# A state-space convolution gated by a GLU, forward and gradients: 8 KB pieces of SBUF for all phases, the down product over all channels in one pass, its gradient transposed at once, part of the weight transposes moved forward

## The chip, the cores and the metric

The kernel runs on one core of one Trainium2 chip. The time is the device time of one execution in microseconds (us), given as the median of three runs. A profile, with a trace of every instruction, comes from one further execution. The engines are named as the profile does: PE (matrix products), DVE (elementwise), ACT (activations, copies, casts), POOL (elementwise work and issuing stores and the convolution's loads) and SP (issuing the other loads).

## The reference

Everything is for one sequence of S = 2048 positions, D = 1024 channels, F = 3584 hidden features, in bf16. The output is computed, and the gradients of nine inputs for a given grad_out.

```
xn = layernorm(x)                                  # x is A_q
kv = shift_conv(k, shift_k) * v                    # four taps per channel
y  = irfft(rfft(kv, 2S) * rfft(ssm_k, 2S))[:S]     # long convolution per channel
s  = xn * (y + kv * ssm_D)
bm = ((xn @ w_gate) * (xn @ w_up)) @ w_down
out = x + s * silu(bm)
out, vjp = jax.vjp(f, x, k, v, shift_k, ssm_k, ssm_D, w_gate, w_up, w_down)
grads = vjp(grad_out)
```

## The kernel before

The sequence is cut into 16 blocks of 128 rows, the channels into 8 pieces of 128, the features into 28 pieces (fc), two of which make a slab of 256. The long convolution is a Fourier transform written out as matrix products with cosine tables (TF, TFO, TI, from `build_tables`) and elementwise combinations on DVE. It is written as a generator that hands out small units of work, each with an estimated cost; `make_pump` gives a `pump` that takes units until their sum has reached a given fraction of the total, and the product loops call it at every tick. So the convolution runs inside the dense products, at a pace set by counts. Loads go out on SP's queue in the order of the program (`ld`), stores and the convolution's loads on POOL's (`st`, `cld`). Tiles come from pools; a tile whose place is still in use makes its first writer wait.

The stages, with the times that they take in the profiled execution:

- 0 to 187 us: layer norm of the blocks in pieces of 1, 1, 2, 4, 4 and 4 (`layer_norm`, L396; its transposes L438 go through one PSUM buffer, copied by ACT or DVE as the scheduler picks, L439, to XNT). After each group of four blocks (q) follow the gate and up products of fc 0 to 3 (`gu_unit`, L442; product psg L452, casts to gut L454). Then `build_tables` (L140): integer angles, two Sin activations L159 for each of eight pieces, and 64 transposes L166 with copies L167.
- 187 to 706: `gu_unit` for fc 4 to 27, in two halves each. Each unit stores gut to GUTd, multiplies its halves to hT on DVE, stores hT to HTd, and at once transposes hT (L465), copies it (L467) and stores it to Hd. `conv_forward` is pumped inside, and leaves y in YFd.
- 706 to 728: the last unit's hT, w_down's loads, the first ht from HTd.
- 728 to 958: the down product (psbm, L781) in two passes over halves of the channels, so that HTd is read twice; the gating behind it computes the output, dbm (gradient of bm, stored to DBMd), dy and dxa. In the second pass `dy_forward` (transform of dy) is pumped to 7% of the backward convolution. The gradient dD is a product beside it (psd, L826).
- 958 to 1048: w_down is loaded as wrow and transposed (L864); DBMd is loaded again, block by block, and transposed to DBMT (`load_dbmt`, L868 to L874).
- 1048 to 1783: for each slab four `dh_half` (product psdh L886, dht L888, dgt = gul times dht on DVE, stored to DGUTd; its transposes L897 at once, copies L898 to dgu), and `dw_slab` (psdw L904, wb L908, out). `conv_backward` is pumped by `btick`.
- 1783 to 2022: gradient of w_down from Hd and DBMd (psdw L947), the rest of the backward convolution pumped inside.
- 2022 to 2143: w_gate and w_up are loaded as wn and transposed (`build_wgu`, L979 to L989), seven pairs of pieces, each followed by its part of the first two blocks of dx (psx L1000).
- 2143 to 2486: the other 14 blocks of dx (psx) and layer norm's gradient.

## Time and profile before

| what | us |
|---|---|
| median of three runs | 2481.09 (2480.47 to 2485.43) |
| profiled execution | 2487.35 |
| its span, from first to last instruction | 2485.6 |
| PE busy | 2242.7 |
| DVE busy | 1445.3 |
| ACT busy | 859.8 |
| POOL busy | 626.6 |

The mean granted clock of PE is 0.967 of full speed. The profiled execution is 0.25% longer than the median, so that a duration of the trace may be read beside the runs' times as it stands. In a row of waits, the engine and the instruction that waited stand left of the arrow, what released it right of it, and then the sum, the number and the longest of these waits. In a row of groups the columns are line, engine, operation, tiles and count, then busy time and the mean of one in ns, then the idle time before them and its releaser.

### The profile page before, as it was taken

What the parts mean: (1) busy time and instruction counts of PE and PEld (TensorE: products, weight loads), DVE (VectorE), ACT (ScalarE), POOL (GpSimd) and SP (SyncE); (2) the same over time, 40 slices, a digit from 0 to 9 for tenths busy, and PEclk for the clock granted to TensorE, in tenths of its full rate; (3) what the DMA queues carried; (4) which work ended last, traced back from release to release, by engine and by line L of the source; (5) the groups of instructions that cost most, each with busy time, mean ns of one, the idle gap of its engine ahead of it and who ended that gap; (6) DMA issues with size and microseconds to landing.
All of it is one profiled execution on the core that took longest, in us unless ns stands there. A gap on an engine that the chain in (4) does not pass through costs nothing.

```text
span 2485.6 us, 35847 instructions
## 1 busy us (share of the span) xinstructions
PE 2242.7 (90%) x14634; PEld 1190.7 (48%) x14634; DVE 1445.3 (58%) x1935; ACT 859.8 (35%) x1204; POOL 626.6 (25%) x963
## 2 busy tenths in 40 slices
PE   3778999999979894799999999999999978999997
PEld 1335566666634442545454555444554434444443
DVE  6348979796855585526966775676674531322212
ACT  4573444444422221533343443345432112311111
POOL 2352223222213332022344344422213310000000
PEclk9889999999989997899999999999999989999999
DMA  8335656645569998534566665644747556433221
GB/s 244 130 117 207 223 189 208 200 164 177 195 229 331 325 324 223 182 130 164 181 211 217 205 213 184 199 155 158 278 150 233 181 163 204 161 122 140 103 101 34
DMA packets 217541, 469.55 MB, mean 189 GB/s; under 512 B 37488, under 2 KB 126616, under 8 KB 205344
## 3 DMA queue, kind: packets, MB, share of 16 engines
q0 software_dynamic: 71392, 265.92, 31.0%
q1 hardware_dynamic: 141824, 199.25, 25.2%
q8 instruction: 114, 1.87, 0.3%
q10 hardware_dynamic: 4160, 2.10, 0.3%
q14 instruction: 51, 0.42, 0.0%
HBM read 277.36 MB, written 194.02 MB: 190 GB/s over the span
## 4 chain that ended last, share of the span: by engine, by line
issue 37%; PE 30%; DVE 14%; DMA 9%; POOL 7%; ACT 3%; POOLq 0%; SPq 0%; DVEq 0%; ACTq 0%
PE psdw L904 12%; PE psbm L781 4%; PE psdw L947 4%; DVE W L179 4%; PE psdh L886 2%; POOL out_dram L60 2%; DMA wrow<-DBMd 2%; PE tr L897 1%; DVE m L179 1%; DVE dgt L179 1%; POOL HTd L60 1%; DMA DGUTd<-dgt 1%; DMA B<-HFd 1%; DVE HX L179 1%; PE psg L452 1%
## 5 line engine op out<-in xcount | busy, mean ns | idle before, releaser
L452 PE MATMUL psg<-XNT,wslab 128*128 128x512 bf16 x1792 | 417.8, 387 | 4.4 <-ACT XNT L439 4.4
L904 PE MATMUL psdw<-dgu,XN 128*128 128x512 bf16 x1792 | 402.6, 379 | 0.0
L1000 PEld LDWEIGHTS <-dgut 128*128 128x128 bf16 x1792 | 174.9, 98 | 222.2 <-DMA dgut<-DGUTd 15.2
L452 PEld LDWEIGHTS <-wslab 128*128 128x128 bf16 x1792 | 174.0, 100 | 198.6 <-issue 20.8
L904 PEld LDWEIGHTS <-XN 128*128 128x128 bf16 x1792 | 172.2, 98 | 192.1 <-issue 0.3
L60 POOL DMA_DIRECT2D out_dram<-wb x280 | 152.4, 551 | 274.0 <-ACT wb L908 198.8
L886 PE MATMUL psdh<-DBMT,wdt 128*128 128x512 bf16 x896 | 217.0, 386 | 2.6 <-ACT dht L888 1.5
L179 DVE TENSOR_TENSOR W<-W 128x512 f32<-128x512 f32 (+1 forms) x272 | 213.2, 784 | 7.1
L781 PE MATMUL psbm<-wd,ht 128*128 128x512 bf16 x896 | 203.2, 384 | 8.9 <-DMA ht<-HTd 6.6
L454 ACT CAST gut<-psg 128x512 bf16<-128x512 f32 x224 | 131.3, 587 | 214.8 <-PE psg L452 210.9
L947 PE MATMUL psdw<-DBMT,dgu 128*128 128x512 bf16 x896 | 198.4, 379 | 6.3 <-ACT wb L950 6.2
L179 DVE TENSOR_TENSOR W<-W,psP 128x512 f32<-128x512 f32 x192 | 122.5, 682 | 123.3 <-PE psP L228 76.2
L1000 PE MATMUL psx<-WGU,dgut 128*128 128x512 bf16 x768 | 169.5, 379 | 0.0
L908 ACT CAST wb<-psdw 128x512 bf16<-128x512 f32 x112 | 65.7, 587 | 247.0 <-PE psdw L904 210.8
L898 ACT COPY dgu<-tr 128x1024 bf16<-128x1024 bf16 x112 | 113.4, 1012 | 100.0 <-PE tr L897 99.4
L179 DVE TENSOR_TENSOR dxn<-psx,dxna_t 128x1024 f32<-128x1024 f32 x16 | 19.6, 1224 | 217.9 <-PE psx L1000 217.8
L947 PEld LDWEIGHTS <-dgu 128*128 128x128 bf16 x896 | 87.5, 98 | 110.4 <-issue 9.2
L781 PEld LDWEIGHTS <-ht 128*128 128x128 bf16 x896 | 87.3, 99 | 110.2 <-issue 7.4
L1000 PE MATMUL psx<-XN,dgut 128*128 128x512 bf16 x512 | 117.9, 387 | 14.4 <-DMA dgut<-DGUTd 14.4
L886 PEld LDWEIGHTS <-wdt 128*128 128x128 bf16 x896 | 85.2, 99 | 88.4 <-issue 7.6
L179 DVE TENSOR_TENSOR dgt<-gul,dht 128x2048 bf16<-128x2048 bf16 x56 | 68.3, 1220 | 98.9 <-ACT dht L888 93.4
L179 DVE TENSOR_TENSOR m<-A,B 128x2048 bf16<-128x2048 bf16 x64 | 75.8, 1221 | 85.4 <-DMA B<-KFd 40.8
(216 smaller groups left out, 3128.8 us busy)
## 6 DMA issues: line engine op xcount, KB each, us to landing
ht<-HTd SPq DMA_DIRECT2D x16, 1792.0 KB, 7.8
gul<-GUTd SPq DMA_DIRECT2D x56, 512.0 KB, 4.8
DGUTd<-dgt POOLq DMA_DIRECT2D x56, 512.0 KB, 5.9
dgut<-DGUTd SPq DMA_DIRECT2D x8, 3584.0 KB, 11.9
GUTd<-gut POOLq DMA_DIRECT2D x48, 512.0 KB, 3.7
A<-DYFd POOLq DMA_DIRECT2D x16, 1024.0 KB, 5.6
out_dram<-wb POOLq DMA_DIRECT2D x224, 64.0 KB, 2.1
dgu<-Hd SPq DMA_DIRECT2D x28, 512.0 KB, 4.7
```

What stands on the lines that cost most here:

```text
L60: return nc.gpsimd.dma_start(out=out, in_=in_)
L179: V.tensor_tensor(o, a, b, op)
L452: nc.tensor.matmul(ps[:], w[:, dc, a, fi * P:(fi + 1) * P], XNT[q][:, dc, :], start=(dc == 0), stop=(dc == DC - 1))
L454: nc.scalar.copy(out=gut[:, a, k * 512:(k + 1) * 512], in_=ps[:])
L781: nc.tensor.matmul(ps[:], ht[:, fc, i * P:(i + 1) * P], wds[fc // 4][:, fc % 4, :], start=(fc == 0), stop=(fc == NF - 1))
L886: nc.tensor.matmul(ps[:], wdt[:, dc, fi * P:(fi + 1) * P], DBMT[:, dc, s0:s0 + 512], start=(dc == 0), stop=(dc == DC - 1))
L897: nc.tensor.transpose(ps[:, i, :], dgt[:, a, i * P:(i + 1) * P], ident[:])
L898: nc.scalar.copy(out=dgu[:, :, a, fi * P:(fi + 1) * P], in_=ps[:])
L904: nc.tensor.matmul(ps[:].rearrange("p a f -> p (a f)"), XN[:, b, dc * P:(dc + 1) * P], dgus[b // 8][:, b % 8].rearrange("p a f -> p (a f)" ...
L908: nc.scalar.copy(out=wb[:], in_=ps[:])
L947: nc.tensor.matmul(ps[:], h[:, fi, b, :], DBM[:, b, dh * 512:(dh + 1) * 512], start=(b == 0), stop=(b == NB - 1))
L1000: nc.tensor.matmul(ps[:, dh * 512:(dh + 1) * 512], t[:, a, 4 * j + f, i * P:(i + 1) * P], WGU[j][:, a, f, dh * 512:(dh + 1) * 512], start= ...
```

## The change

Memory: four pieces of 8 KB a partition (U0 to U3) stand through the kernel, seven more (U4 to U10) from the end of the gate and up products on. XNT, the seven pieces of w_down, DBMT, XN, dgu, DBM and the transposed weights are all views of them, where each phase had its own pool.

Start: the loads of x all go out ahead of the copies KSLd<-k; layer norm's transposes have four PSUM buffers and their copies are DVE's; the tables are built beside the units of q = 1, from one Sin, one Abs and one Sin for each piece instead of two Sins and an integer mask; the second half of the products of fc 24 to 27 is done as a group.

Transposes of hT (and, later, of dgt) are put off: they are kept in a list and written out by `flush` behind the next product.

Down product: both halves of the channels in one pass, two matmuls for each weight load, HTd read once; gating on whole rows; dbm is transposed to DBMT from SBUF, behind the next block's 15th feature piece. `dy_forward` and the dD product go to the backward convolution, where the latter is a product of dyx and kvx for each channel piece. `load_dbmt` is gone. The pump's target for the backward convolution is reached at 0.94 of the ticks, and its total goes from 658 to 664 units.

End: half of the 14 pieces of transposed weights are built beside the last three slabs of w_down's gradient, the rest between the parts of the first two blocks of dx; dgut is loaded in two halves.

Three places in the order of instructions. **SP, the program's start**: x are loads of the blocks of layer norm (1024 elements a row are one block, 4096 four), KSLd the copies of k. Before:

```order
L57 DMA x_136<-in_A_q_dram 128x1024
L57 DMA x_141<-in_A_q_dram 128x1024
L57 DMA KSLd<-in_A_k_dram 2048x128 x5
L57 DMA x_229<-in_A_q_dram 128x2048
L57 DMA x_469<-in_A_q_dram 128x4096
L57 DMA KSLd<-in_A_k_dram 2048x128 x3
L57 DMA x_688<-in_A_q_dram 128x4096
L57 DMA x_907<-in_A_q_dram 128x4096
```

And now:

```order
L57 DMA x_147<-in_A_q_dram 128x1024
L57 DMA x_149<-in_A_q_dram 128x1024
L57 DMA x_151<-in_A_q_dram 128x2048
L57 DMA x_153<-in_A_q_dram 128x4096
L57 DMA x_155<-in_A_q_dram 128x4096
L57 DMA x_157<-in_A_q_dram 128x4096
L57 DMA KSLd<-in_A_k_dram 2048x128 x8
```

All of x stands ahead of the copies of k now. **ACT, building the tables** (TF and TFO from the angles mm, TI from transposes in PSUM; gut and h belong to gate and up units, junk to layer norm). Before, behind the last units of q = 3:

```order
L454 CAST gut<-psg 128x512
L159 ACTIVATE TFO<-mm,negpi 128x4x256
L167 COPY TI<-tr 128x1024
L159 ACTIVATE TFO<-mm,negpi 128x4x256
L167 COPY TI<-tr 128x1024
L159 ACTIVATE TFO<-mm,negpi 128x4x256
```

And now, behind the units of q = 1:

```order
L472 CAST gut<-psg 128x512
L165 ACTIVATE TFO<-ab__743,mhpi 128x4x256
L162 ACTIVATE TFO<-mm,negpi 128x4x256
L164 ACTIVATE ab__751<-mm,negpi 128x1024
L173 COPY TI<-tr 128x1024
L165 ACTIVATE TFO<-ab__751,mhpi 128x4x256
L162 ACTIVATE TFO<-mm,negpi 128x4x256
L164 ACTIVATE ab__759<-mm,negpi 128x1024
```

The sines now stand before the casts of q = 2 and q = 3, with one Abs for every two. **SP, from the down product to the products behind it** (gul are loads of GUTd for dgt, wrow those of w_down or DBMd that are transposed). Before:

```order
L57 DMA kv_t<-KVd 128x4x256
L57 DMA XN<-XNd 128x4096 x3
L57 DMA wrow<-in_B_w_down_dram 128x1024 x2
L57 DMA gul<-GUTd 128x2x1024 x2
L57 DMA wrow<-DBMd 128x1024
L57 DMA XN<-XNd 128x4096
L57 DMA wrow<-DBMd 128x1024 x9
```

And now:

```order
L57 DMA x_t<-in_A_q_dram 128x1024
L57 DMA U_113<-XNd 128x4096
L57 DMA U_114<-XNd 128x4096
L57 DMA U_115<-XNd 128x4096
L57 DMA U_116<-XNd 128x4096
L57 DMA wrow<-in_B_w_down_dram 128x1024 x4
L57 DMA gul<-GUTd 128x2x1024 x6
```

The sixteen loads of DBMd are gone from the row, and four loads of XN stand ahead of the first wrow where there were three. The core of the diff:

```diff
-                mm = tg.tile([P, 2, 4, 256], I32, name="mm")
-                nc.vector.tensor_single_scalar(mm[:, 1], m[:], 8191, ALU.bitwise_and)
-                nc.vector.tensor_scalar(m[:], mm[:, 1], 6144.0, None, op0=ALU.add)
-                nc.vector.tensor_single_scalar(mm[:, 0], m[:], 8191, ALU.bitwise_and)
+                mm = tg.tile([P, 4, 256], I32, name="mm")
+                nc.vector.tensor_single_scalar(mm[:], m[:], 8191, ALU.bitwise_and)
                 dst = T[:, 2 * hf:2 * hf + 2].rearrange("p r c k f -> p k (r c) f")
-                for k in range(2):
-                    nc.scalar.activation(dst[:, k], mm[:, k], ACT.Sin, bias=negpi[:], scale=2.0 * np.pi / 8192.0)
+                sc = 2.0 * np.pi / 8192.0
+                nc.scalar.activation(dst[:, 1], mm[:], ACT.Sin, bias=negpi[:], scale=sc)
+                ab_ = tg.tile([P, 4, 256], F32, name="ab_")
+                nc.scalar.activation(ab_[:], mm[:], ACT.Abs, bias=negpi[:], scale=sc)
+                nc.scalar.activation(dst[:, 0], ab_[:], ACT.Sin, bias=mhpi[:], scale=1.0)
...
-    fa = pool("fa", 1, side="right")
-    XNT = [fa.tile([P, DC, 512], BF16, name=f"XNT{q}") for q in range(4)]
+    ua = pool("ua", 1, side="right")
+    U = [ua.tile([P, 4096], BF16, name=f"U{i}") for i in range(4)]
+    def u8(i, pat="p (a x) -> p a x", **kw):
+        return U[i][:].rearrange(pat, **kw)
+    XNT = [u8(q, a=DC) for q in range(4)]
     fw = pool("fw", 2, side="right")
     fg = pool("fg", 2, side="right")
     ps_gu = pool("ps_gu", 2, space=PSUM)
     ps_tr = pool("ps_tr", 1, space=PSUM)
     ps_y = pool("ps_y", 1, space=PSUM)
-    ps_cv = pool("ps_cv", 2, space=PSUM)
-    lnp = pool("lnp", 2)
+    ps_st = pool("ps_st", 4, space=PSUM)
+    lnp = pool("lnp", 1)
...
-            ps = ps_tr.tile([P, DC, P], BF16, name="tr")
+            ps = ps_st.tile([P, DC, P], BF16, name="tr")
             for dc in range(DC):
                 nc.tensor.transpose(ps[:, dc, :], x4[:, i, dc * P:(dc + 1) * P], ident[:])
-            nc.any.tensor_copy(XNT[q][:, :, qi * P:(qi + 1) * P], ps[:])
+            V.tensor_copy(XNT[q][:, :, qi * P:(qi + 1) * P], ps[:])
...
+    later = []
+    def flush():
+        while later:
+            later.pop(0)()
...
+                flush()
                 tick()
...
-        ps = ps_tr.tile([P, 8, P], BF16, name="tr")
-        for i in range(nb):
-            nc.tensor.transpose(ps[:, i, :], hT[:, i * P:(i + 1) * P], ident[:])
-        h = fg.tile([P, 8, P], BF16, name="h")
-        nc.scalar.copy(out=h[:, 0:nb, :], in_=ps[:, 0:nb, :])
-        st(Hd[fc, :, 4 * qs[0]:4 * qs[0] + nb, :], h[:, 0:nb, :])
+        def turn():
+            ps = ps_tr.tile([P, 8, P], BF16, name="tr")
+            for i in range(nb):
+                nc.tensor.transpose(ps[:, i, :], hT[:, i * P:(i + 1) * P], ident[:])
+            h = fg.tile([P, 8, P], BF16, name="h")
+            nc.scalar.copy(out=h[:, 0:nb, :], in_=ps[:, 0:nb, :])
+            st(Hd[fc, :, 4 * qs[0]:4 * qs[0] + nb, :], h[:, 0:nb, :])
+        later.append(turn)
...
-    x4 = ln_load(0, 1)
-    slabs = [load_slab(0, nc.scalar)]
-    xs = [(0, 1, x4)]
-    for (b0, n) in ((1, 1), (2, 2)):
-        xs.append((b0, n, ln_load(b0, n)) if b0 == 1 else (b0, n, None))
     nop = lambda: None
-    for (b0, n, x4) in xs:
-        if x4 is None:
-            x4 = ln_load(b0, n)
-        layer_norm(b0, n, x4)
-    slabs.append(load_slab(1, nc.scalar))
-    build_bcast(ps_y)
-    for fc in range(4):
-        gu_unit(fc, [0], slabs[fc // 2], nop)
-    for q in range(1, 4):
-        x4 = ln_load(4 * q, 4)
-        layer_norm(4 * q, 4, x4)
-        for fc in range(4):
-            gu_unit(fc, [q], slabs[fc // 2], nop)
-    lns.release()
-    lnp.release()
+    slabs = [load_slab(0, nc.scalar), load_slab(1, nc.scalar)]
+    chunks = [(0, 1), (1, 1), (2, 2), (4, 4), (8, 4), (12, 4)]
+    xs = [(b0, n, ln_load(b0, n)) for (b0, n) in chunks]
     for ds in range(8):
         ld(KSLd[ds, 3:3 + S, :].rearrange("(p a) d -> p a d", a=16),
            kin[:, ds * P:(ds + 1) * P].rearrange("(p a) d -> p a d", a=16))
-    build_tables(ps_tr)
+    for c in xs[:3]:
+        layer_norm(*c)
+    for q in range(4):
+        if q > 0:
+            layer_norm(*xs[q + 2])
+        for fc in range(4):
+            gu_unit(fc, [q], slabs[fc // 2], nop)
+        if q == 0:
+            build_bcast(ps_y)
+        if q == 1:
+            build_tables(ps_st)
+    lns.release()
+    lnp.release()
+    ps_st.release()
+    ps_cv = pool("ps_cv", 2, space=PSUM)
...
-    w = None
-    for fc in range(4, NF):
+    for fc in range(4, NF - 4):
         if fc % 2 == 0:
             w = load_slab(fc // 2, nc.sync)
         for hf in range(2):
             gu_unit(fc, [2 * hf, 2 * hf + 1], w, tick)
+    slabs = [load_slab(NSL - 2, nc.sync), load_slab(NSL - 1, nc.sync)]
+    for hf in range(2):
+        for fc in range(NF - 4, NF):
+            gu_unit(fc, [2 * hf, 2 * hf + 1], slabs[(fc - NF + 4) // 2], tick)
+    flush()
...
+    ub = pool("ub", 1, side="right")
+    U += [ub.tile([P, 4096], BF16, name=f"U{i}") for i in range(4, 11)]
...
+            ps = ps_y.tile([P, 4, P], F32, name="psY")
+            for b in range(NB):
+                nc.tensor.matmul(ps[:, 0, :], x[:, b, :], kv[:, b, :], start=(b == 0), stop=(b == NB - 1))
+            yield 0.1
+            dt_ = cs.tile([P, P], F32, name="dt_")
+            tt(dt_[:], ps[:, 0, :], ident_f[:], MUL)
+            dr_ = cs.tile([P, 1], F32, name="dr_")
+            V.tensor_reduce(dr_[:], dt_[:], AX.X, ADD)
+            V.tensor_copy(ddo[:, ds:ds + 1], dr_[:])
+            yield 0.7
...
-    for dh in range(2):
-        hsl = slice(dh * 512, (dh + 1) * 512)
-        wds = []
-        for j in range(7):
-            wd = mw.tile([P, 4, 512], BF16, name="wd")
-            ld(wd[:], B_w_down[j * 512:(j + 1) * 512, hsl].rearrange("(c p) d -> p c d", p=P))
-            wds.append(wd)
-        psd = ps_dd.tile([P, 4, P], F32, name="psd")
-        for bp in range(8):
-            c, r0 = divmod(2 * bp, 8)
-            ht = mh.tile([P, NF, 256], BF16, name="ht")
-            ld(ht[:], HTd[bp])
-            bm = mt.tile([P, 2, 512], BF16, name="bm")
-            for i in range(2):
-                ps = ps_bm.tile([P, 512], F32, name="psbm")
-                for fc in range(NF):
-                    nc.tensor.matmul(ps[:], ht[:, fc, i * P:(i + 1) * P], wds[fc // 4][:, fc % 4, :],
-                                     start=(fc == 0), stop=(fc == NF - 1))
...
+    WD = [u8(j, a=4) for j in range(7)]
+    for j in range(7):
+        ld(WD[j], B_w_down[j * 512:(j + 1) * 512, :].rearrange("(c p) d -> p c d", p=P))
+    DBMT = [u8(7 + q, a=DC) for q in range(4)]
+    def bm_mm(ps, ht, i, fc):
+        for dh in range(2):
+            nc.tensor.matmul(ps[:, dh * 512:(dh + 1) * 512], ht[:, fc, i * P:(i + 1) * P],
+                             WD[fc // 4][:, fc % 4, dh * 512:(dh + 1) * 512], start=(fc == 0), stop=(fc == NF - 1))
+    def gate(b, ps):
...
+        nc.scalar.copy(out=bm, in_=ps[:])
+        nc.scalar.activation(sig, bm, ACT.Sigmoid)
+        nc.scalar.activation(sgn, bm, ACT.Sigmoid, scale=-1.0)
...
+        def turn():
+            ps = ps_tr.tile([P, DC, P], BF16, name="tr")
+            for dc in range(DC):
+                nc.tensor.transpose(ps[:, dc, :], dbm[:, dc * P:(dc + 1) * P], ident[:])
+            nc.scalar.copy(out=DBMT[b // 4][:, :, (b % 4) * P:(b % 4 + 1) * P], in_=ps[:])
+        later.append(turn)
+    def load_ht(bp):
+        ht = mh.tile([P, NF, 256], BF16, name="ht")
+        ld(ht[:], HTd[bp])
+        return ht
+    ht = load_ht(0)
+    pss = [ps_bm.tile([P, D], F32, name="psbm") for i in range(2)]
+    for fc in range(NF):
+        for i in range(2):
+            bm_mm(pss[i], ht, i, fc)
+    for i in range(2):
+        gate(i, pss[i])
+    for bp in range(1, 8):
+        ht = load_ht(bp)
+        for i in range(2):
+            ps = ps_bm.tile([P, D], F32, name="psbm")
+            for fc in range(NF):
+                bm_mm(ps, ht, i, fc)
+                if fc == 14:
+                    flush()
+            gate(2 * bp + i, ps)
...
-    BT = NSL * (8 + 16) + 7 * 16.0
+    BT = 0.94 * (NSL * (8 + 16) + 7 * 16.0)
     def btick(n):
         bcnt[0] += n
-        bpump(0.07 + 0.93 * bcnt[0] / BT)
+        bpump(bcnt[0] / BT)
...
-    def load_dbmt(b):
-        t = bw.tile([P, D], BF16, name="wrow")
-        ld(t[:], DBMd[:, b, :])
-        ps = ps_tr.tile([P, DC, P], BF16, name="tr")
-        for dc in range(DC):
-            nc.tensor.transpose(ps[:, dc, :], t[:, dc * P:(dc + 1) * P], ident[:])
-        nc.any.tensor_copy(DBMT[:, :, b * P:(b + 1) * P], ps[:])
...
+        def turn():
+            for a in range(2):
+                ps = ps_tr.tile([P, 8, P], BF16, name="tr")
+                for i in range(8):
+                    nc.tensor.transpose(ps[:, i, :], dgt[:, a, i * P:(i + 1) * P], ident[:])
+                nc.scalar.copy(out=dgu[:, :, a, fi * P:(fi + 1) * P], in_=ps[:])
+        later.append(turn)
...
     wdt = load_wdt(0)
+    flush()
+    for q in range(4):
+        ld(XN[q], XNd[:, 4 * q:4 * q + 4, :])
+    nd = 0
     for sl in range(NSL):
-        if sl == 0:
-            for b in range(8):
-                load_dbmt(b)
         dgus = []
         for hf in range(2):
-            dgu = bq.tile([P, 8, 2, SLW], BF16, name="dgu")
+            dgu = u8(4 + nd % 3, "p (b a f) -> p b a f", b=8, a=2)
+            nd += 1
             for fi in range(2):
                 dh_half(2 * sl + fi, hf, wdt, dgu)
-                if sl == 0 and hf == 0 and fi == 0:
-                    for b in range(8, 16):
-                        load_dbmt(b)
             dgus.append(dgu)
-        if sl == 0:
-            for q in range(4):
-                ld(XN[:, 4 * q:4 * q + 4, :], XNd[:, 4 * q:4 * q + 4, :])
         if sl + 1 < NSL:
             wdt = load_wdt(sl + 1)
+        flush()
         dw_slab(sl, dgus)
...
+    for sp in range(NSL - 3):
+        dwd_slab(sp, nop)
     bdrain()
-    for p_ in (ps_tr, ps_dw, ps_dh, ps_y, ps_c3, bq, bg, bw):
+    tip.release()
+    gw = pool("gw", 1)
+    gn = pool("gn", 2)
+    gd = pool("gd", 1)
+    stores = [u8(i, a=4) for i in range(4)] + [gw.tile([P, 4, D], BF16, name=f"W{i}")[:] for i in range(3)]
+    def early():
+        for n in range(7):
+            yield from build_wgu(n, stores[n], gn, ps_tr)
+    eg = early()
+    ec = [0, 0]
+    def side():
+        ec[0] += 1
+        while ec[1] < 28 * ec[0] / 12.0:
+            ec[1] += 1
+            next(eg, None)
+    for sp in range(NSL - 3, NSL):
+        dwd_slab(sp, side)
+    run(eg)
...
+    for n in range(14):
+        if n >= 7:
+            run(build_wgu(n, u8(n - 3, a=4), gn, ps_tr))
```

214 lines of the change are left out of this document (92 added, 122 removed).

## The prediction, made before the changed kernel had run

> **What bounds the kernel now.** I read the page first, for the engine that fills the span and for its clock.
>
> ```profile
> span 2485.6 us, 35847 instructions
> PE 2242.7 (90%) x14634; PEld 1190.7 (48%) x14634; DVE 1445.3 (58%) x1935; ACT 859.8 (35%) x1204; POOL 626.6 (25%) x963
> PEclk9889999999989997899999999999999989999999
> ```
>
> PE is busy for 90%, and no other engine for more than 58%. The clock row dips in a few slices only. So PE's matmuls set the length, and what a change can win is the time in which PE stands still or runs at a lower clock. The matmuls are the same ones before and after (reloaded and re-transposed tiles replace others one for one), so the sum is made of losses, stage by stage. I cut the span at the stage borders (columns: PE, PEld, DVE, ACT and POOL busy, then granted clock, DMA share, GB/s).
>
> ```profile
> core 0: us, PE busy (x) PEld busy (x) DVE busy (x) ACT busy (x) POOL busy (x), PEclk, DMA share, GB/s
> 0.00:48.00 48.00, 9.84 (x42) 4.22 (x43) 28.93 (x73) 22.06 (x36) 9.69 (x22) 1.00 0.82 234
> 48.00:187.00 139.00, 105.52 (x574) 52.75 (x574) 59.63 (x104) 81.00 (x114) 58.89 (x74) 0.84 0.43 141
> 187.00:706.00 519.00, 494.79 (x4446) 311.17 (x4445) 434.40 (x561) 218.04 (x336) 132.20 (x199) 0.99 0.57 194
> 706.00:728.00 22.00, 7.37 (x74) 6.22 (x72) 9.46 (x13) 3.94 (x6) 3.10 (x4) 0.65 0.98 348
> 728.00:958.00 230.00, 220.95 (x1224) 106.70 (x1222) 147.11 (x237) 56.23 (x76) 77.86 (x111) 0.97 0.86 301
> 958.00:1048.00 90.00, 45.78 (x386) 30.85 (x384) 51.00 (x79) 32.21 (x40) 10.63 (x15) 0.72 0.70 193
> 1048.00:1783.00 735.00, 701.56 (x4512) 364.81 (x4510) 465.72 (x544) 304.60 (x415) 258.14 (x409) 1.00 0.57 190
> 1783.00:2022.00 239.00, 232.65 (x1135) 110.57 (x1133) 144.79 (x201) 56.15 (x76) 65.98 (x113) 1.00 0.57 184
> 2022.00:2143.00 121.00, 94.27 (x729) 54.01 (x728) 23.79 (x36) 32.46 (x34) 1.44 (x2) 0.90 0.63 190
> 2143.00:2486.00 343.00, 330.01 (x1530) 149.41 (x1527) 80.52 (x92) 53.09 (x75) 8.67 (x16) 0.99 0.30 108
> ```
>
> PE's busy time by the clock is about what the work of a row needs at full clock; the row's length less that is its loss. At 48 to 187 it is 139 - 105.52 x 0.84 = 50; at 958 to 1048, 90 - 45.78 x 0.72 = 57; at 2022 to 2143, 121 - 94.27 x 0.90 = 36; the first 48 us lose 48 - 9.84 = 38. The long rows lose little for their length: 519 - 494.79 = 24 and 735 - 701.56 = 33 stand idle. What PE waits for says why (total us, times, longest; the hT row is for 187 to 706, the others for the whole span).
>
> ```profile
> PE tr L438 <- DVE x L435: 15.9, 1, 15.9
> PE tr L438 <- DVE sq_b L427: 14.1, 1, 14.1
> PE tr L438 <- ACT XNT L439: 11.0, 10, 1.1
> PE tr L465 <- DVE hT L179: 20.1, 24, 4.1
> PE tr L873 <- DMA wrow<-DBMd: 24.9, 5, 19.4
> PE tr L897 <- DVE dgt L179: 23.4, 23, 3.6
> PE psx L1000 <- DMA dgut<-DGUTd: 14.4, 2, 12.3
> PE tr L988 <- DMA wn<-in_B_w_up_dram: 10.9, 12, 2.2
> ```
>
> The change reaches every one of these. PE's own pitch, from a stretch without gaps, is 23.09 / 107 = 216 ns for a 512-wide matmul:
>
> ```profile
> 1056.55 23.09 PE psdw L904 x107
> ```
>
> **The change part by part.** Each term is made against the profiled execution, 2487.35 us (span 2485.6 and 1.75 around it).
>
> Term 1, start and tables (0 to 187, loss 38 + 50 = 88). The third piece of x now waits behind five 512 KB copies on SP's queue:
>
> ```profile
> 1.64 17.00 SPq L57 DMA_DIRECT2D KSLd<-in_A_k_dram  x5
> 18.82 10.13 DMA x<-in_A_q_dram
> 48.35 6.01 PE L452 MATMUL psg<-XNT,wslab 128*128 128x512 bf16 x15 [1.10 <-ACT XNT L439]
> 155.00:175.00 20.00, 11.57 (x92) 7.54 (x90) 10.95 (x15) 18.27 (x22) 10.82 (x10) 0.78 0.30 88
> ```
>
> With all six loads of x ahead of those copies, x should land some 10 us sooner, but DVE now does the 4.4 us sum over the next four blocks before it finishes these, so I count 6 us. The tables are built at 155 to 175, where PE has 11.57 us of work at clock 0.78: about 11 us lost. Now they are built beside the gate and up units of q = 1. There they cost ACT (busy us, mean ns):
>
> ```profile
> L159 ACT ACTIVATE TF<-mm,negpi 128x1024 bf16<-128x1024 int32 x8 | 9.2, 1151 | 2.1 <-DVE mm L154 2.0
> L167 ACT COPY TI<-tr 128x1024 bf16<-128x1024 bf16 x8 | 8.0, 1005 | 0.2
> L439 ACT COPY XNT<-tr 128x1024 bf16<-128x1024 bf16 x16 | 16.2, 1013 | 19.3 <-PE tr L438 19.3
> L989 DVE COPY WGU<-tr 128x1024 bf16<-128x1024 bf16 x12 | 8.3, 691 | 31.6 <-PE tr L988 31.6
> L159 ACT ACT_TABLE_LOAD x1 | 1.3, 1283 | 0.0
> ```
>
> Sixteen sines become sixteen sines and eight Abs: 24 x 1.15 = 28 us, and 8 us of copies; some 45 us of ACT with q = 1's own casts, over about 28 us of PE's work. So ACT sets that stretch and eats part of the gain. In return the copies behind layer norm's transposes go to DVE (1.01 to 0.69 us), over four buffers instead of one, which removes most of the 11.0 us that PE waits for them (ten times), and the loads of q = 2 and 3 are done early. I take 18 us for this: **-24**, between -40 (the whole stretch near PE's pace) and 0 (ACT's table work takes it all back).
>
> Term 2, the transposes of hT one product later (187 to 706). The order of PE's rows puts on average 0.57 us more matmuls (at 216 ns) between the unit's last product and them. Against 24 waits of 20.1 us in all that is 24 x 0.57 = 14 at most and 0 at least, since the longest, 4.1, are queues on DVE: **-6**.
>
> Term 3, 706 to 728. The first ht waits for the last HTd store, and then takes its own time:
>
> ```profile
> 716.57 11.19 DMA ht<-HTd
> 957.26 1.28 SPq L57 DMA_DIRECT2D XN<-XNd  x3
> 958.59 9.30 DMA wrow<-in_B_w_down_dram
> 969.00 25.32 DMA wrow<-DBMd
> ht<-HTd SPq DMA_DIRECT2D x16, 1792.0 KB, 7.8
> ```
>
> Now seven 1 MB pieces of w_down go ahead of it. Two of them can load early; about five, with ht, come at the 348 GB/s of that row: 20 us, against 22 today. **-2**, -6 to +4.
>
> Term 4, the down product in one pass (728 to 958, idle 9.1, and 0.03 of 220.95 by the clock: 16). Half of ht's sixteen loads go (8 x 1.792 MB), so the DMA share of 0.86 falls; dy_forward and the dD product leave; gating is the same work for DVE, which was busy 147 of 230 us with dy_forward in it. The added transposes of dbm (128 at about 56 ns, 7 us) were there at L873 and only move. **-11**; -16 if all is hidden, 0 if a new gating chain holds a psum buffer.
>
> Term 5, 958 to 1048 (loss 57). The 25.32 us trip of DBMd through memory goes, and with it the 24.9 us wait. What is late next is wrow. Today it takes 9.30 us, behind 3 MB of XN; in the new order four XN loads of 1 MB stand ahead, issued as the last block frees each piece. I leave that wait (958.59 + 9.30 - 957.26 = 11 us), about 8 for the low clock behind it (the row loses 45.78 x 0.28 = 13 so today), and 8 for the last block's gating and for dgt's load: 27 left, **-30**; -40 if the wait hides, -10 if the queue of XN and the late gating add up. The Trainium skill, "DMA: Bandwidth & Descriptors", section "Queues, rings and completion order", says that an engine takes the descriptors of one ring in ring order; that speaks against this part of the change, and the 9.30 us agree. By it, wrow is the last of 4.5 MB.
>
> Term 6, 1048 to 1783. Transposes of dgt one product later: by the order 0.73 us more cover, against 23 waits of 23.4 us, some -10. But the convolution's backward part must now run all its 664 units (of which 46 came before this stage) in 0.94 of the ticks, 15% denser, with dy_forward's DVE work in it: 465.72 / 735 = 63% becomes some 73%. What DVE waits for there is ACT and PE, not itself:
>
> ```profile
> DVE dgt L179 <- ACT dht L888: 83.9, 16, 31.9
> DVE yl L179 <- ACT yl L693: 54.1, 6, 10.9
> ```
>
> So I give 3 back: **-7**, from -15 to +25 (each wait for dgt doubled).
>
> Term 7, early weight transposes in the last three dwd slabs: 28 groups on 12 steps through one psum buffer, so 16 of them wait for the copy of the one ahead (0.69 or 1.01 us, less overlap): **+6**, 0 to 15.
>
> Term 8, 2022 to 2143 (loss 36). Half of the fourteen pieces are then built, and dgut's halves are loaded before: 14.4 us go, half of the 10.9 and much of the low clock; 10 stay. **-26**, -15 to -30.
>
> The sum is -24 - 6 - 2 - 11 - 30 - 7 + 6 - 26 = -100. From 2487.35 that gives 2387; the median shown, 2481.09, lies 6 below the profiled execution, so the forecast for the median is **2381 us**.
>
> On the clock: what follows a gap runs slow in the rows (0.65, 0.72, 0.84). The Trainium skill, "TensorE: Matmul & The Clock Gate", Part 1, says that about 3.4 us of idle time halve it; the rows agree in kind, and by it each gap that shrinks below that also saves the slow time after it, which would put terms 1, 5 and 8 at their far ends.
>
> **The rivals.** (a) **ACT sets the start**: 45 us of table work in q = 1 come back in full, term 1 is 0: 2405. For it, ACT's 18.27 of 20 us at 155 to 175; against it, its 16 us of copies go to DVE. (b) **wrow behind XN**: term 5 gives 10: 2401. For it, the 9.30 us; against it, that XN's pieces come free up to 10 us before the product's end. It is the case that the ring rule above makes likelier. (c) **the gaps close wholly**, clock and all: -40 - 14 - 6 - 16 - 40 - 15 + 0 - 30 = -161, 2320, and half way to it 2350. (d) **the backward convolution is already at its own pace** (slower): it did 612 units between 1005 and 2022, 0.60 a us; if its chain of loads, products and DVE cannot go faster, 664 take 1100 us, and with the last steps that no longer overlap (27 ticks of 2.3 us) the stage takes 1161 instead of 1013: +148. The other terms give -93: 2536. It decides below about 0.63 units a us. For it, POOL's and DVE's waits for loads and PE; against it, PE idles only 33 us there, DVE 37%. (e) **it does little of what it says**: the order moves the transposes by 0.6 to 0.7 us only, starts move by 6, and new waits take the rest: within 0.2%.
>
> **How the numbers follow.** Forecast 0.51, (a) 0.12, (b) 0.15, (c) 0.13, (d) 0.07, (e) 0.02. The forecast's own bounds, taken in quadrature, are about 35 either way; with (a), (b) and half of (c) the range is 2335 to 2440. About 0.2% is what a measurement of this kernel can tell from no change. Faster 0.91, within it 0.02, slower 0.07.
>
> **What would show it.** Term 1: the first psg at 40 to 43 us, and no stretch of mere table transposes as at 155 to 175. Term 5: no transposes fed from DBMd, the first psdw 25 to 35 us behind the last psbm, wrow landing 8 to 11 behind it. Term 6: PE idle below 35 us in the dh and dw stage, and DVE near 73%. Term 8: no wait for dgut in the first block of dx. It is wrong if the conv's last unit comes after the dwd products (PE then idles at the end of them), if ACT stays full to beyond 120 us, or if gating holds a psbm buffer.

## The result, and the profile after

The changed kernel takes 2397.81 us (median of four runs, 2396.9 to 2399.34) beside 2483.26 for the kernel before on the same occasions: a ratio of 0.9657, interval 0.964 to 0.9673. That is 85 us less, where 100 were forecast; 2398 lies inside the range of 2335 to 2440. The profiled execution's span went from 2485.6 to 2395.3.

The page of the changed kernel, as quoted for the kernel before:

```profile
span 2395.3 us, 35474 instructions
PE 2206.5 (92%) x14370; PEld 1185.8 (50%) x14634; DVE 1443.0 (60%) x1941; ACT 863.7 (36%) x1197; POOL 590.7 (25%) x923
PEclk9899999999989999999999999999999999999999
```

And its stages, cut at the same points of the work (columns: PE, PEld, DVE, ACT, POOL busy, clock, DMA share, GB/s):

```profile
0.00:34.00 34.00, 9.43 (x42) 4.11 (x43) 27.14 (x75) 18.31 (x35) 5.06 (x17) 1.00 0.99 297
34.00:158.50 124.50, 98.60 (x638) 53.74 (x649) 75.13 (x115) 81.55 (x115) 67.94 (x88) 0.92 0.61 201
158.50:671.40 512.90, 487.26 (x4299) 307.24 (x4370) 424.55 (x551) 214.24 (x332) 126.94 (x190) 0.99 0.56 188
671.40:693.80 22.40, 7.82 (x68) 6.78 (x68) 9.43 (x13) 3.76 (x6) 3.11 (x4) 0.59 1.00 371
693.80:903.00 209.20, 204.19 (x995) 93.71 (x1016) 105.74 (x167) 61.62 (x61) 37.99 (x60) 0.99 0.66 229
903.00:940.30 37.30, 25.62 (x199) 16.43 (x202) 19.07 (x31) 16.25 (x21) 7.76 (x12) 0.86 0.77 266
940.30:1722.00 781.70, 727.84 (x4841) 393.96 (x4931) 562.41 (x703) 318.82 (x435) 267.39 (x426) 0.99 0.59 194
1722.00:1978.00 256.00, 246.59 (x1307) 121.59 (x1331) 126.23 (x181) 75.89 (x98) 65.34 (x111) 0.99 0.63 202
1978.00:2050.00 72.00, 69.35 (x487) 38.14 (x495) 12.40 (x18) 19.73 (x22) 0.54 (x1) 1.00 0.61 203
2050.00:2395.00 345.00, 329.79 (x1505) 150.05 (x1534) 80.88 (x92) 53.52 (x76) 8.65 (x16) 0.99 0.29 102
```

Work that moved between stages makes lengths alone misleading, so I count the work of each stage from its weight loads (their records are nearly complete in both traces; some matmul records are missing in this one, 14370 against 14634) by the pitch of the matmul that each feeds: 216 ns for 512 columns, 109 for 256, 56 for 128. The trace has, for example, 1.95 us for 32 transposes 128 wide and 1.04 us for 8 products 256 wide. Length less work is the loss: idle time, low clock, and what PE is busy beyond that pitch, as between products of different kinds. In the dh and dw stage before, 33 of the 56.4 us are idle time.

| term | loss before | loss after | difference | forecast |
|---|---|---|---|---|
| 1, start and tables | 98.6 | 65.4 | -33.2 | -24 |
| 2, gate and up | 37.4 | 35.7 | -1.7 | -6 |
| 3, handover to the down product | 17.4 | 18.5 | +1.1 | -2 |
| 4, down product | 18.7 | 9.4 | -9.3 | -11 |
| 5, handover to dh and dw | 58.6 | 15.4 | -43.2 | -30 |
| 6, dh and dw | 56.4 | 78.5 | **+22.1** | **-7** |
| 7, w_down's gradient | 5.7 | 11.2 | +5.5 | +6 |
| 8, first blocks of dx | 35.9 | 3.1 | -32.8 | -26 |
| rest | 13.1 | 14.5 | +1.4 | 0 |

The differences add up to -90.1, the spans differ by 90.3. So the account is closed, and of the terms that were forecast at more than 2 us one has the wrong sign. (The medians differ by 85 and not by 90 because the profiled execution of the kernel before, 2487.35, lies 4 us above its median here, and that of the changed kernel, 2397.11, does not.) The down product has 896 weight loads in both traces, one for each of its matmuls: the order with two matmuls behind one another on the same weights saves the second reading of HTd, but no weight load. The PE waits of the changed kernel that matter here, over the whole span:

```profile
PE tr L925 <- DVE dgt L185: 31.5, 18, 5.5
PE tr L486 <- DVE hT L185: 29.9, 31, 3.4
PE psY L137 <- DVE row L132: 18.0, 1, 18.0
PE psdw L933 <- ACT wb L937: 9.3, 3, 7.8
PE tr L172 <- ACT TI L173: 7.9, 3, 3.1
PE tr L898 <- DMA wrow<-in_B_w_down_dram: 6.0, 1, 6.0
PE tr L981 <- DMA wn<-in_B_w_up_dram: 1.2, 2, 1.0
```

The waits for x, DBMd and dgut are gone, that for wn fell from 10.9 to 1.2. But dgt, whose transposes were put off, is waited for longer than before (31.5 against 23.4, in 18 waits instead of 23). The row of psY is the time from the start to PE's first product, whose input DVE now copies at 18.1; in the kernel before PE began after a wait of 14.1 us for sq_b. New is the wait for ACT's wb in the dw product. The wait for TI is as long as before (7.7 us there) but of another kind: six waits of at most 1.6 us have become three of up to 3.1, and they now stand ahead of layer norm's transposes.

Both, wb and TI, can be followed. At 1135.7 PE stops for 7.8 us. On ACT's line of the trace, and in the table of DMA issues for 1115 to 1150 (count, KB each, median us to landing), stands why:

```profile
1127.53 0.59 ACT L937 CAST wb<-psdw 128x512 bf16<-128x512 f32 x1 [1.14 <-PE psdw L933]
1142.94 1.07 ACT L937 CAST wb<-psdw 128x512 bf16<-128x512 f32 x2 [14.83 <-DMA out_dram<-wb]
out_dram<-wb POOLq DMA_DIRECT2D x8, 64.0 KB, 8.0
out_dram<-ddo POOLq DMA_DIRECT2D x1, 2.0 KB, 20.1
```

A cast waits 14.8 us for a store of wb ahead of it, and these stores, 2 us otherwise, stand behind the store of dD, which takes 20.1 us for 2 KB. It writes ddo, 128 partitions by 8, transposed: 1024 single values. In the kernel before the same store took 23.0 us, right at the handover of term 5.

The row of TI is the tables. PE's transposes of TF stand in its queue ahead of layer norm's for q = 2, and wait for ACT:

```profile
82.57 1.14 ACT L164 ACTIVATE ab__751<-mm,negpi 128x1024 f32<-128x1024 int32 x1
83.61 1.01 ACT L173 COPY TI<-tr 128x1024 bf16<-128x1024 bf16 x1
84.50 1.16 ACT L165 ACTIVATE TFO<-ab__751,mhpi 128x1024 bf16<-128x1024 f32 x1
...
88.69 1.01 PE L172 MATMUL tr<-ident,TF 128*128 128x128 bf16 x8 [3.10 <-ACT TI L173]
92.71 1.01 PE L172 MATMUL tr<-ident,TF 128*128 128x128 bf16 x8 [3.01 <-ACT TI L173]
94.66 3.66 PE L450 MATMUL tr<-ident,x 128*128 128x128 bf16 x32 [0.94 <-ACT TI L173]
99.09 5.34 PE L470 MATMUL psg<-U,wslab 128*128 128x512 bf16 x23 [0.78 <-DVE U L451]
```

From 80.5 to 97.2 ACT does nothing but table work, and PE has no psg between 78 and 99.

### The profile page after: what moved, and what is told of

It is laid out like the page before. It is cut to its first block, busy times and chain, and to the rows that moved or that the text cites. A ratio compares the mean times of both kernels' runs of the same rounds, so it can differ in the third digit from the quotient of the medians.

```text
span 2395.3 us, 35474 instructions
## 1 busy us (share of the span) xinstructions
PE 2206.5 (92%) x14370; PEld 1185.8 (50%) x14634; DVE 1443.0 (60%) x1941; ACT 863.7 (36%) x1197; POOL 590.7 (25%) x923
## 4 chain that ended last, share of the span: by engine, by line
PE 41%; issue 25%; DVE 13%; DMA 9%; POOL 6%; ACT 5%; another core or an unknown queue 0%; POOLq 0%; SPq 0%; ACTq 0%; DVEq 0%
PE psx L1049 12%; PE psdw L933 10%; PE psdw L993 5%; PE psg L470 3%; DVE W L185 3%; DMA out_dram<-wb 2%; PE psdh L911 2%; DVE m L185 2%; POOL out_dram L60 2%; PE tr L925 2%; DMA DGUTd<-dgt 1%; PE psbm L808 1%; DVE HX L185 1%; PE tr L981 1%; DMA HFd<-HX 1%
## 5 line engine op out<-in xcount | busy, mean ns | idle before, releaser
L470 PE MATMUL psg<-U,wslab 128*128 128x512 bf16 x1709 | 406.6, 385 | 9.1 <-DVE U L451 3.6
L933 PE MATMUL psdw<-U,U 128*128 128x512 bf16 x1737 | 400.3, 380 | 14.7 <-ACT wb L937 9.3
L1049 PE MATMUL psx<-U,dgut 128*128 128x512 bf16 x1376 | 305.6, 379 | 1.7
L933 PEld LDWEIGHTS <-U 128*128 128x128 bf16 x1792 | 172.8, 98 | 199.2 <-issue 9.5
L911 PE MATMUL psdh<-U,wdt 128*128 128x512 bf16 x857 | 210.2, 383 | 5.2 <-ACT dht L913 3.3
L808 PE MATMUL psbm<-U,ht 128*128 128x512 bf16 x875 | 196.9, 382 | 7.7 <-DMA ht<-HTd 6.4
L993 PE MATMUL psdw<-U,U 128*128 128x512 bf16 x873 | 199.3, 380 | 3.5 <-ACT wb L996 1.4
L926 ACT COPY U<-tr 128x1024 bf16<-128x1024 bf16 x112 | 113.4, 1013 | 84.6 <-PE tr L925 84.4
L993 PEld LDWEIGHTS <-U 128*128 128x128 bf16 x896 | 86.7, 98 | 100.7 <-issue 2.8
L1065 ACT ACTIVATE junk<-dxn 128x1024 bf16<-128x1024 f32 x16 | 16.9, 1057 | 279.7 <-DVE dxn L185 279.7
L185 DVE TENSOR_TENSOR m<-A,B 128x2048 bf16<-128x2048 bf16 x64 | 75.8, 1221 | 63.6 <-DMA B<-KFd 27.1
L60 POOL DMA_DIRECT2D out_dram<-dx_t x16 | 8.6, 540 | 402.0 <-DVE dx_t L1077 402.0
```

Source lines behind the costliest of these rows:

```text
L60: return nc.gpsimd.dma_start(out=out, in_=in_)
L185: V.tensor_tensor(o, a, b, op)
L470: nc.tensor.matmul(ps[:], w[:, dc, a, fi * P:(fi + 1) * P], XNT[q][:, dc, :], start=(dc == 0), stop=(dc == DC - 1))
L808: nc.tensor.matmul(ps[:, dh * 512:(dh + 1) * 512], ht[:, fc, i * P:(i + 1) * P], WD[fc // 4][:, fc % 4, dh * 512:(dh + 1) * 512], start=(f ...
L911: nc.tensor.matmul(ps[:], wdt[:, dc, fi * P:(fi + 1) * P], DBMT[2 * hf + k][:, dc, :], start=(dc == 0), stop=(dc == DC - 1))
L926: nc.scalar.copy(out=dgu[:, :, a, fi * P:(fi + 1) * P], in_=ps[:])
```

## The experiments

Twelve kernels ran, called e1 to e12 here. Ratios are to the kernel before (the changed kernel: 0.9657); each ratio has runs of the kernel before from its own occasion, so ratios are compared, and 0.001 is 2.5 us.

**Is it the store of dD?** First I moved it in the program (e1 is the changed kernel, e2 the kernel before).

```diff
-        st(o_dD.rearrange("(c p) -> p c", p=P), ddo[:])     # end of dy_forward
...
     run(eg)
+    st(o_dD.rearrange("(c p) -> p c", p=P), ddo[:])         # behind w_down's gradient
```

> The changed kernel with one DMA moved: the 2 KB store of dD is issued behind the last products of w_down's gradient instead of in the middle of the first slab. Theory S (that store keeps the store queue from landing anything): in the changed kernel's trace it takes 20.1 us to land (1122.3 to 1142.5), the 64 KB stores of wb behind it land at 1142.7 to 1143.2, and PE stands 7.8 us with 10.2 us of half clock behind it. Without it this gap goes: 7.8 + 5.1 = 13 us less, some 2385 (at least 8 less), and the gap before psdw there disappears. Rival (the 1 MB store of DYFd issued just ahead, 18.1 us, is what is slow): the gap stays, time within 3 us of 2398.

> The kernel before with the same DMA moved: the store of dD behind the last backward product instead of right behind the down product. The first re-read of DBMd took 25.32 us there (969.00 to 994.3), issued 0.1 us behind that store, which itself landed at 991.9. Theory S (the store is what held it): wrow<-DBMd lands in under 10 us, and the time falls by 12 to 20 us, to 2463 to 2471. So that much of the gain in the handover from 958 to 1048 would not have come from leaving out the re-read. Rival R (the re-read itself is slow, since it waits for the stores of DBMd and shares the queue with 4 MB of XN): the first wrow<-DBMd still takes over 20 us and the time stays within 4 us of 2483.

Ratios 0.9655 (0.9635 to 0.9675) and 0.9998 (0.9985 to 1.0011): nothing. But the edits hadn't done what they say either. The store was issued at 1122.9 and landed at 1141.8 in the one, issued at 973.5 and landed at 994.2 in the other: it went out as soon as ddo was there, wherever it was written. These two settle nothing on the theory, and serve as repeats of the two kernels. So I changed the store itself (e5 is the changed kernel, e6 the kernel before).

```diff
+        ps = ps_y.tile([P, 4, P], F32, name="psY")
+        nc.tensor.matmul(ps[0:8, 0, :], ddo[:], ident[:], start=True, stop=True)
+        drow = cx.tile([P, NB, P], BF16, name="dyx")
+        V.tensor_copy(drow[0:8, 0, :], ps[0:8, 0, :])
-        st(o_dD.rearrange("(c p) -> p c", p=P), ddo[:])
+        st(o_dD.rearrange("(c p) -> c p", p=P), drow[0:8, 0, :])
```

> The changed kernel with dD turned by one product with the identity before it is stored, so that the store writes 8 rows of 256 bytes instead of 1024 single values; one more matmul, one small copy. Moving the store later in the program had left it at the same place in the queue (issued at 1122.9, landed at 1141.8), so this takes its cost away where it stands. Theory S (the scattered store keeps the stores behind it from landing, and ACT's casts of wb and then PE wait for these): the store lands in under 6 us, PE's gap of 7.4 to 7.8 us before psdw at 1136 and the 10.2 us of half clock behind it go: 8 to 13 us less than 2398, 2385 to 2390. Rival (the DYFd store ahead of it, or the channel's own state, is slow): the gap stays, within 4 us.

> The kernel before with the same store of dD in rows, at the end of the down product. Theory S: the first wrow<-DBMd, 25.3 us and 22.95 us in two executions, lands in under 10 us, PE's waits for it fall from 24.9 to under 10 us and the time by 10 to 18 us, to 2463 to 2471. Then that part of the handover's gain is the store's place, not the re-read that was left out. Rival R (the re-read itself): over 18 us, within 4 us of 2481.

In the changed kernel the store of 8 rows landed in 3.9 us, and the stores of wb around it in 1.8 at the median:

```profile
out_dram<-wb POOLq DMA_DIRECT2D x14, 64.0 KB, 1.8
out_dram<-dyx POOLq DMA_DIRECT2D x1, 2.0 KB, 3.9
```

PE's wait for wb in that stage is down from 9.3 to 1.5 us. The 1 MB store of DYFd issued just ahead, which the rival took for the cause, landed in 5.0 us instead of 18.1: it had been held up too. The ratio is 0.9632 (0.9613 to 0.9652), 6 us under the changed kernel's, with intervals that still touch; the trace is clearer, where the stage from first to last psdw went from 781.6 to 773.0 us. Theory S holds there, a little smaller than I had it. In the kernel before the ratio is 0.9964 (0.995 to 0.9977), 9 us, just short of the 10 to 18 expected, and its PE waits have

```profile
PE tr L877 <- DMA wrow<-DBMd: 5.8, 5, 1.9
```

where 24.9 us stood. So most of the wait that the prediction put down to the trip of DBMd through memory was another DMA's, and the change did not remove that DMA: it moved it into term 6. One reservation: SP's row came out in another order in e6 (two loads of gul, 1 MB, now go out behind the first two of DBMd instead of ahead), so that a part of the 19 us may be theirs.

**The delay of dgt's transposes.** First they are written at once again (e3).

```diff
-        later.append(turn)
+        turn()                     # in dh_half
```

> The changed kernel with the transposes of dgt written at once again, as in the kernel before, and nothing else undone. Theory D (the delay helps, and the denser convolution ate it): slower by 8 to 20 us, PE's waits for dgt rise from 31.5 to 45 us or more. Rival N (PE waits for DVE's queue, which is some 8 us long when dgt stands behind a convolution's unit, so that one product more of cover changes little): within 5 us of 2398, waits for dgt 30 to 38 us.

Ratio 0.9678 (0.9647 to 0.9709), 5 us above, not clear of the changed kernel's interval. The loss of the stage, counted as above, is 87.2 instead of 78.5. The waits for dgt are 35.3, inside what the rival gave. Between the two theories it is undecided: the stage loses some 9 us more in one trace, and the times differ by perhaps 5, less than D said. Nor is all of the 9 dgt's: within the stage its waits rise only from 27.1 to 30.5, while PE waits 13.1 us for ACT's W, 7.7 of them behind a cast that waited 10.0 us for a store of wb, so the store of dD shows there under another name than the 9.3 for wb in the changed kernel. That execution, 2408.23, was also one of the longer ones (2393.58 to 2409.07). Then the other side, dgt ahead of its tick (e4):

```diff
             flush()
-            btick(1)
+            if k == 0:
+                btick(1)
...
         later.append(turn)
+        btick(1)
```

> The changed kernel with dgt's multiply written ahead of the convolution units of its second tick instead of behind them. Theory N (dgt stands in DVE's queue behind convolution work: from 1376 to 1385 and from 1549 to 1559 some ten multiplies ran between the last dht and dgt): PE's waits for dgt fall from 31.5 to under 18 us and the time by 6 to 15 us, to 2383 to 2392. Rival D (the waits come from too little PE work between the last psdh and the transposes, not from DVE's order): waits for dgt within 5 us of 31.5 and the time within 4 us of 2398.

Ratio 0.9672 (0.9652 to 0.9693), waits for dgt 35.4: theory N's numbers fail, and the rival's nearly hold. But theory N was not put to the test: dgt begins on average 1.16 us behind the last cast that it needs, where it was 1.15 in the changed kernel, so the edit hardly moved it. The order in which it is written doesn't decide this place in DVE's queue. What does stand there is plain in the changed kernel, the last cast of dht it needs having ended at 1379.9:

```profile
1379.40 0.68 DVE L185 TENSOR_TENSOR yl<-yl,dyl 128x1024 bf16<-128x1024 bf16 x1
...
1381.21 0.68 DVE L185 TENSOR_TENSOR kshl<-kshl,yl 128x1024 bf16<-128x1024 bf16 x1
1381.81 1.28 DVE L188 SCALAR_TENSOR_TENSOR B<-W 128x512 bf16<-128x512 f32 x2
1383.61 0.69 DVE L185 TENSOR_TENSOR dyl<-dyl,Dbc 128x1024 bf16<-128x1024 bf16 x1 [0.51 <-DMA dyl<-DYd]
1384.22 1.29 DVE L188 SCALAR_TENSOR_TENSOR B<-W 128x512 bf16<-128x512 f32 x2
1385.42 1.22 DVE L185 TENSOR_TENSOR dgt<-gul,dht 128x2048 bf16<-128x2048 bf16 x1
1386.70 1.03 PE L925 MATMUL tr<-ident,dgt 128*128 128x128 bf16 x8 [5.52 <-DVE dgt L185]
```

Five and a half microseconds of the convolution's multiplies run before dgt, one of them after waiting for a load. This is one of the longest cases; in half of the 56 multiplies dgt begins within 0.7 us of its cast.

**The density of the convolution (e7).**

```diff
-    BT = 0.94 * (NSL * (8 + 16) + 7 * 16.0)
+    BT = (NSL * (8 + 16) + 7 * 16.0)
```

> The changed kernel with the pump's factor 0.94 back at 1, so that the convolution's units are spread over all ticks, 6% thinner. Theory P (the density of the convolution sets the waits for dgt and the loss of 78 us in the stage of dh and dw): waits for dgt fall from 31.5 to 20 to 27 us, the stage gains 5 to 12 us, and the some 36 units that are left when the early weight transposes start are drained there for 10 to 25 us: 2400 to 2415 in all. Rival (the waits come from single long units, not from density): waits for dgt 29 to 34 us, and the whole 2408 to 2425 from the drain.

Ratio 0.9797 (0.9779 to 0.9815), 35 us slower, above what either gave. In the stage it gains: 763.1 us instead of 781.6, loss 63.9. That is not all density, since PE did not wait for wb in this execution; against the kernel with dD in rows (loss 69.8) it is 6 us. Waits for dgt are 32.5 over the whole span (31.5 in the changed kernel) and 28.5 in the stage (27.1): they don't come from density, as the rival said. The price is at the end, in the stretch from 1968 to 2011 between w_down's gradient and dx:

```profile
1968.00:2011.00 43.00, 20.06 (x168) 17.03 (x168) 0.69 (x1) 20.03 (x21) 0.54 (x1) 0.54 0.70 226
```

The convolution's last product ends 12 us later (1922.9 instead of 1910.4), the first early transpose starts 25 us later (1944.8 instead of 1920.3), and what is left of them is done there alone, at half the clock. So 0.94 is what makes the early transposes fit.

**The tables (e8).** The call of `build_tables` goes behind the loop over q:

```diff
-        if q == 1:
-            build_tables(ps_st)
+    build_tables(ps_st)
     lns.release()
```

> The changed kernel with the tables written behind the units of q = 3 again. Theory T (most of the start's gain is the overlap of the tables with gate and up units): the point at which 512 products of fc 0 to 3 and the tables are done moves from 133 us to 143 to 155 us, the whole slower by 8 to 18 us, 2406 to 2416. Rival X (the gain is x's loads, 48 to 34 us to the first product, and the tables overlap anyway wherever they are written): within 5 us of 2398.

It is faster, against both theories: ratio 0.9577 (0.9561 to 0.9593), 20 us under the changed kernel. The very same instructions now stand further apart: ACT does one or two of them between casts, and transposes and copies of x go ahead of those of the tables.

```profile
80.41 1.16 ACT L164 ACTIVATE ab__1177<-mm,negpi 128x1024 f32<-128x1024 int32 x1
81.64 0.59 ACT L472 CAST gut<-psg 128x512 bf16<-128x512 f32 x1
82.13 0.59 ACT L488 COPY h<-tr 128x512 bf16<-128x512 bf16 x1
82.60 1.16 ACT L165 ACTIVATE TFO<-ab__1177,mhpi 128x1024 bf16<-128x1024 f32 x1
83.65 0.59 ACT L472 CAST gut<-psg 128x512 bf16<-128x512 f32 x1
...
34.00:138.50 104.50, 91.46 (x624) 49.07 (x634) 73.04 (x116) 79.36 (x113) 69.88 (x88) 1.00 0.72 238
```

The same point of the work (the counts of weight loads differ by 1 us of work) is reached at 138.5 instead of 158.5, at full clock throughout (1.00 against 0.92). ACT's busy time is nearly the same, 79 against 82 us; what differs is who stands behind it.

**Together, and the rest of the start and the end.** All four of the next have the tables late and dD in rows.

> The changed kernel with both edits that made it faster: the tables written behind q = 3 again, and dD stored in rows. If the two act in different stages (the tables before 160 us, the store at 1120 to 1145), the gains of 24 and 8 us add up: 2362 to 2370. If the store's gap was partly hidden by what the tables change (a later conv, another state of DVE's queue), 2370 to 2378.

Ratio 0.9546 (0.9529 to 0.9563), 2366.46 us: 27.5 under the changed kernel by the ratios, the two parts of 20 and 6 added up.

The second has the delayed transposes one product later again:

```diff
-                flush()
+                if k == 0 and a == 1:
+                    flush()                # gu_unit
                 tick()
...
-            flush()
+            if k == 1:
+                flush()                    # dh_half
             btick(1)
```

> The kernel of e9 with the delayed transposes written two products behind their unit instead of one, for hT and dgt. Theory C (cover: PE needs some more us of products between a unit and its transposes, since DVE's queue is 5 to 8 us long there): waits for hT fall from 26 to under 12 us, for dgt from 28 to under 12, the time by 10 to 25 us against e9. Rival (the scheduler puts the transposes where it wants, or DVE's late multiply delays the next product through its buffers): waits within 5 us, the time within 4 us of e9.

Ratio 0.9473 (0.9457 to 0.9489), 2347.84 us: 18 us under the kernel with the two edits, and the fastest of all. PE's waits in e9 and then in e10:

```profile
PE tr L928 <- DVE dgt L185: 34.6, 21, 5.7
PE tr L486 <- DVE hT L185: 23.8, 33, 2.2
...
PE tr L930 <- DVE dgt L185: 18.7, 10, 4.6
PE tr L487 <- DVE hT L185: 13.5, 15, 2.8
```

Each fell by 10 to 16 us, that is by somewhat under half, and not to under the 12 expected. The theory of cover stands in kind: these waits are a queue on DVE of up to 6 us, and one product (1.7 us) does not span it. Part came back as other waits: the stage of dh and dw is only 4.7 us shorter in the trace (774.1 to 769.4), for PE now waits 7.7 us for wb and 5.1 for the copies behind the transposes there, and in gate and up the waits for KX rose from 5.6 to 14.0. Whether yet more delay gains was not tried.

The third leaves out the early transposes of weights:

```diff
-            ec[1] += 1
-            next(eg, None)
...
-        if n >= 7:
-            run(build_wgu(n, u8(n - 3, a=4), gn, ps_tr))
+        run(build_wgu(n, u8(n - 3, a=4) if n >= 7 else stores[n], gn, ps_tr))
```

> The kernel of e9 with all fourteen pieces of weights transposed between the parts of the first two blocks of dx, as in the kernel before, and none beside w_down's gradient. The prediction had +6 for the early ones and -26 for what they, and the earlier load of dgut, save behind. Theory W (the early transposes carry most of it): slower than e9 by 10 to 20 us. Rival L (the two halves of dgut, loaded early, carry it): slower by 5 us at most.

Ratio 0.9553 (0.9532 to 0.9573): no difference from e9. w_down's gradient ends at 1927.3 instead of 1947.4, and dx makes up for it. With all fourteen pieces built in the first blocks of dx, PE waits there for

```profile
PE psx L1041 <- DMA dgut<-DGUTd: 2.4, 1, 2.4
PE tr L984 <- DMA wn<-in_B_w_up_dram: 1.5, 2, 1.1
```

and no longer for 14.4 and 10.9 us. So the early transposes, their price in term 7 included, gain nothing that can be measured. By the waits that went, it is the loads that carry term 8 (dgut in halves, and the places of dgut and wn free earlier); no run took these out, together or apart.

The fourth puts the loads of x back among the copies of k:

```diff
-    xs = [(b0, n, ln_load(b0, n)) for (b0, n) in chunks]
+    xs = [(b0, n, ln_load(b0, n)) for (b0, n) in chunks[:2]]
+    ksl(range(5))                   # five of the copies KSLd<-k
+    xs += [(b0, n, ln_load(b0, n)) for (b0, n) in chunks[2:4]]
+    ksl(range(5, 8))
+    xs += [(b0, n, ln_load(b0, n)) for (b0, n) in chunks[4:]]
```

> The kernel of e9 with the loads of x in the old order among the copies of k: the third piece behind five copies, the last two behind all eight. Theory X (this order alone moved the first product from 48 to 34 us): first psg at 44 to 50 us, slower than e9 by 8 to 14 us. Rival (layer norm's copies on DVE through four buffers and the warm activation table did it): first psg under 40 us, slower by 4 us at most.

Ratio 0.959 (0.9574 to 0.9607), 11 us slower than e9, and the first product stands at 47.49 instead of 34.3 us, behind a wait of 16.95 us for x. Theory X holds.

## Why the prediction came out as it did

Sign and range held, and six of the eight terms came out within their own bounds; 5 and 8 went past their good ends. The forecast was 15 us too good in the difference. Of these, 5 are the profiled executions' distance from the medians; the other 10 are term 6, 29 us off, partly paid back by 1, 5 and 8. So part of the hit is luck: large errors of both signs.

**Term 6** was the step that failed: "some -10" for the delay, "3 back" for the density, -7 in all; it measured +22, near the end of +25 that the range allowed. The -10 was at the upper end of what the run without the delay shows (9 in the trace, 5 in the times). The 3 should have been 6 (the thinner pump against dD in rows). What was missing altogether is the store of dD, 9 us, which the change part did not price: it named dD's product as leaving the down product and never asked where its store would land and what stands behind it on POOL's queue. These three bring 56.4 to between 62 and 66, not to 78.5; the remaining 12 to 16 us are open. DVE's share there is 72% (562.41 of 781.70; 73% was forecast), and its queue ahead of dgt is long, but no run took dy_forward's work out of the stage by itself. PE's idle time there, forecast below 35 us, is 54.

**Term 5** came out at -43 instead of -30. wrow, behind the four loads of XN, made PE wait 6.0 us, not 11, so rival (b) did not come about. It was not the order that changed: the four pieces of XN landed at 896.8, 900.7, 904.2 and 907.9, and wrow, issued at 903.1, at 909.0, right behind the last. These landings agree with the rule of the Trainium skill that the prediction cites ("DMA: Bandwidth & Descriptors", section "Queues, rings and completion order"). The wait was shorter because the loads of XN went out from 891.9 on, 11 us before the last psbm ended. The stores behind that of dD on POOL's queue landed in their order too, with 14.8 us for the cast that waits behind them. But the loads that stood still beside it in the kernel before were on SP's queue, so the order within one queue does not explain those; why they did is open. And "the trip of DBMd" was credited with 24.9 us, most of which, by e6, belonged to the store of dD beside it; its 9 us of time (e6) returned in term 6 (e5, 6 us). Without this shift both terms would have been nearer their forecasts.

**Term 1**, -33 where -24 was forecast, is two large effects of opposite sign. The first product came at 34.0, not 40 to 43, since the order of x's loads alone moves it by 13 us and the time by 11 (e12). The prediction had two things wrong here. The third piece of x landed at 9.2 us instead of 29.0, twice the some 10 us that were counted. And DVE's sum over the next four blocks, counted as a new cost, stood ahead of layer norm's end in the kernel before as well, and still does:

```profile
32.38 4.41 DVE L400 TENSOR_REDUCE ssum<-x 128x4 f32<-128x4096 bf16 x1
...
23.26 4.40 DVE L412 TENSOR_REDUCE ssum<-x 128x4 f32<-128x4096 bf16 x1
```

Against that, rival (a)'s mechanism is real and costs 20 us (e8, e9): ACT sets the stretch from 80 to 97. What neither forecast nor rival had is the remedy: the tables were taken for an amount of ACT work, 45 us, and it is their place in the queues that costs, for ACT is as busy in the faster version.

**Term 8**, -33 with -30 as its good end, came for a reason that is only half right: the waits for dgut and wn went, as said; building half of the pieces early brought nothing (e11), and with it **term 7**, its price of 5.5, bought nothing that the times show. **Terms 2 and 4**: -1.7 and -9.3 against -6 and -11; hT's waits from 187 to 706 fell from 20.1 only to 16.8 us, by 24 waits again, since one product more is short against DVE's queue (e10).

Of the signs that were named ahead, these came: no transposes fed from DBMd, no wait for dgut, DVE near 73%, and the convolution's last product (1910.4) ahead of the end of w_down's gradient. These did not: the first psdw stands 37 us behind the last psbm (25 to 35 were named), and wrow landed 6 us behind it (8 to 11).

Rival (c), the gaps closing wholly at 2320 to 2350, is about what the changed kernel with three further edits reaches (2348). Rival (d) did not come: the convolution ended in time with 15% more units per tick, PE idle for 54 us there. On the clock, the row at 903 to 940 has 0.86 where 958 to 1048 had 0.72, and that at 1978 to 2050 has 1.00 for 0.90: shorter gaps, less slow time behind them. That agrees with the rule of the Trainium skill, "TensorE: Matmul & The Clock Gate", Part 1, that the prediction cites.

## What to carry to other kernels

Before a DMA is moved, look how long it takes to land where it stands and what waits behind it: a wait's name in the profile may be that of the victim, and the price then moves along with its cause. Work that an engine can do at any time before a deadline was best written late here and left to fill gaps; written early, the same instructions stood in front of others. A delay between producer and consumer has to be as long as the queue that it spans; one product here did little, two took away somewhat under half of the waits. And before an edit's result is read, look in the trace whether the instruction moved: for three of the twelve (e1, e2, e4) it had not.
